# Last expert weights, left-half stores, the slot cast and the first q/k loads rearranged in an attention + soft-MoE kernel

## The chip, the cores and the metric

The kernel runs on one core of a Trainium2 chip. A core has five engines, each with its own in-order instruction queue: TensorE (PE, matmuls; its weight loads are shown as PEld), VectorE (DVE), ScalarE (ACT), GpSimd (POOL) and SyncE (SP). Transfers run on 16 DMA engines that all queues share. A DMA is issued from the queue of an engine (here GpSimd, ScalarE or SyncE) and runs on its own afterwards. The metric is the device time in microseconds; all times below are us from the first instruction of the profiled execution unless said otherwise.

## The reference

Attention over 4 batches, 8 heads, 768 positions, head size 64. Three heads are causal, five see a window of 64 and 4 first positions. The result, as 3072 tokens of 512 features, goes through a soft mixture of experts: 32 slots, 4 for each of 8 experts.

```python
scores = scale * np.matmul(q, k.transpose(0, 1, 3, 2))
scores = np.where(mask[None, :, :, :], scores, -1000000000.0)
a = np.exp(scores - np.max(scores, axis=-1, keepdims=True))
a = a / (np.sum(a, axis=-1, keepdims=True) + 1e-09)
x = np.matmul(a, v)                       # then (3072, 512)
...
logits = x @ phi                          # 3072 x 32
d = softmax of logits over the tokens;  slot_input = d.T @ x
for e in range(E):                        # 8 experts, 4 slots each
    h = np.maximum(slot_input[e] @ w1[e], 0.0)
    slot_out[e] = h @ w2[e]
c = softmax of logits over the slots
return (c @ slot_out).astype(np.float32)  # 3072 x 512
```

Inputs are float32; the kernel computes in bfloat16 with float32 sums and writes float32.

## The kernel before

The order of instructions on each engine is written out by hand (`manual_schedule`). Work falls into four stages.

**Start.** The first pair of heads of q and k goes by two plain float32 loads into the tile `stage`: q from ScalarE's queue and k from SyncE's (L264). VectorE casts q to bfloat16 and ScalarE casts k (L291, L292), TensorE transposes k and then q, and the two engines bring them back as `Tk` and `Tq`. All later inputs and weights are loaded by GpSimd, which casts to bfloat16 in the transfer; they share one in-order queue: q, k, v of four heads at a time, and between them the sixteen weight matrices w1[0..7], w2[0..7] (`w_load`, L142), 2 MB of float32 each.

**Attention.** Sixteen rounds of one pair of heads (`for n in range(NP)`): scores on TensorE, exp on ScalarE (L185), masks on VectorE (L197), products with v on TensorE (L206), normalization on VectorE. It ends near 110 us.

**Slots and experts.** Logits, slot sums and the first expert layer (L528, w1), the transposes of its result (`turn`), and the second layer. `second(e, xs, spread)` (L560) does w2[e] in eight matmuls for each column half x in `xs`: half 0 is columns 0 to 255 ("left"), half 1 is 256 to 511 ("right"), summed over experts in the PSUM tiles `sp[0]` and `sp[1]`. w2[5], w2[6] and w2[7] go into buffers that attention sets free: w2[5] into the masks', w2[6] and w2[7] into the two buffers of `pT`. `w_half(e, cs)` (L429) loads one column half of w2[e]. GpSimd's queue ends with: w2[5] whole, then left halves of w2[6] and w2[7], then right halves of w2[6] and w2[7]. Each half row of 256 bfloat16 is its own piece of 512 B in the destination.

**Output.** Every partition holds 24 output rows. `product(r, o, cs, t)` multiplies row set r with columns cs of `slot_out` (L584) and scales it out of PSUM: with t == 2 on ScalarE (L586), else on VectorE (L588). Once the left halves of all w2 are in, VectorE casts `sp[0]` to `slot_out[:, left]` (L599), and `half_rows` computes and stores the left half of rows 0 to 7, in groups of 2, 2 and 4 rows, from GpSimd's queue (L596). TensorE then does the right half of w2[6], three filler matmuls (`keep_busy`, L280, on zeros), and the right half of w2[7]. VectorE casts `sp[1]` to `slot_out[:, right]` (L604), and rows 8 to 23 follow whole: row 8 as two halves on both engines, the others in turn on ScalarE (odd rows) and VectorE (even rows), stored from SyncE's queue in groups of 1, 1, 2, 4, 4, 4 rows (L616). Last come the right halves of rows 0 to 7, in two groups of 4, on SyncE's queue. The output tiles lie in the buffers of w1.

Of the kernel before, what the change touches and what calls it, by code (L numbers as in the profile page):

```python
# [10 lines left out]
F32 = mybir.dt.float32  # L11
# [27 lines left out]
def kernel(  # L39
# [13 lines left out]
    nc = tc.nc  # L53
    P = 128
# [3 lines left out]
    NE, DM, F = moe_w1.shape  # L58
# [16 lines left out]
    def single(shape, dt, name, tag=None):  # L75
        return singles.tile(shape, dt, name=name, tag=tag or name)

    w1s = [single([P, 4, F], BF16, f"w1_{e}") for e in range(NE)]
    w2s = [single([P, 8, DM], BF16, f"w2_{e}") for e in range(NE - 3)] + [None] * 3
# [55 lines left out]
    w2v = [moe_w2[e].rearrange("(fi fo) d -> fi fo d", fo=8) for e in range(NE)]  # L135
# [83 lines left out]
    def x_transpose(n, i0=0, i1=6):  # L219
        b, hp = n // 4, n % 4  # L220
        tp = trp.tile([P, S], BF16, tag="tr", name="tpx")
        for i in range(i0, i1):
            nc.tensor.transpose(tp[:, i * 128:(i + 1) * 128], xb[b][:, i, hp * 128:(hp + 1) * 128], ident)  # L223
        nc.vector.tensor_copy(xT[:, hp, i0 * 128:i1 * 128], tp[:, i0 * 128:i1 * 128])  # L224
# [35 lines left out]


    stage = ptp.tile([P, 2, S], F32, tag="pT", name="stage")
    for eng, src, z in ((nc.scalar, q, 0), (nc.sync, k, 1)):
        eng.dma_start(stage[:, z], src[0, 0:2].rearrange("h (p s) d -> (h p) (s d)", s=12))  # L264
    ir32 = is_retrieval.tensor.reshape([H]).bitcast(I32)
    nc.sync.dma_start(ri, bass.AP(tensor=ir32, offset=0, ap=[[0, 1], [1, 2 * H]]))
    raws[0] = raw.tile([P, 2, 2 * S], BF16, tag="raw", name="raw")
# [6 lines left out]
    V = nc.vector  # L274
# [3 lines left out]
    def keep_busy(t, count):  # L278
        for _ in range(count):
            nc.tensor.matmul(t, zero[:, :P], zero, start=True, stop=True)  # L280

    idle = pvp.tile([P, 512], F32, tag="pv", name="idle")
# [55 lines left out]
    for n in range(NP):  # L338
# [18 lines left out]
        m, x = (1, 0) if n == 1 else (n // 2 + 1, n % 2)  # L357
        turns = 0 < n < NP - 2
        b, r = n // 4 - 1, n % 4
# [67 lines left out]
    left, right, full = slice(0, 256), slice(256, 512), slice(0, 512)  # L427

    def w_half(e, cs):  # L429
        nc.gpsimd.dma_start(w2s[e][:, :, cs], w2v[e][:, :, cs])  # L430
# [1 line left out]
    w2s[5] = single([P, 8, DM], BF16, "w2_5", tag="msk")  # L432
    nc.gpsimd.dma_start(w2s[5], w2v[5])
    w2s[6] = ptp.tile([P, 8, DM], BF16, tag="pT", name="w2_6")
    w_half(6, left)


    def bank(t, shape=(P, 512), dt=F32):
        pool, tag = ((scp, "sc"), (trp, "tr"), (pvp, "pv"))[t]
        return pool.tile(list(shape), dt, tag=tag, name="bank")  # L440
# [28 lines left out]
    logits_mm(bl, (0, 1, 2))  # L469
    w2s[7] = ptp.tile([P, 8, DM], BF16, tag="pT", name="w2_7")  # L470
    w_half(7, left)
    for e in (6, 7):
        w_half(e, right)
    x_transpose(last, 0, 3)
    x_transpose(last, 3, 6)
    copies(2, 0)
    idle = bank(2)
# [15 lines left out]
    idle = bank(2)  # L493
# [22 lines left out]
    cs = bank(1, (P, 1))  # L516
# [5 lines left out]
    for e4 in range(2):  # L522
        t = xp.tile([P, 2, 512], BF16, tag="xb", name="hs")
# [26 lines left out]

    spt = [bank(0, (P, 2, 512)) for x in range(2)]
    sp = [t[:, 0, :256] for t in spt]
    idle = spt[1][:, 1]

    def second(e, xs=(0, 1), spread=False):
        e4, g = e // 4, e % 4
        for fo in range(8):
            c = fo % 4 if spread else g
            for x in xs:
                nc.tensor.matmul(sp[x][32 * c:32 * c + 32, :], hT[e4][:, fo, 32 * g:32 * g + 32],  # L560
                                 w2s[e][:, fo, 256 * x:256 * x + 256],
                                 start=(e4 == 0 and fo == 0), stop=(e == 7 and fo >= 4))
# [9 lines left out]
    turn(1)  # L572
    second(4, spread=True)
    second(5, spread=True)
    for e in (6, 7):
        second(e, (0,), spread=True)


    NL = 8
    ov = out.rearrange("(p r) d -> p r d", r=24)  # L580

    def product(r, o, cs, t):
        op = bank(t, (P, cs.stop - cs.start))
        nc.tensor.matmul(op, er[r], slot_out[:, cs], start=True, stop=True)  # L584
        if t == 2:
            nc.scalar.activation(o, op, ACT.Copy, scale=rrow[:, r:r + 1])  # L586
        else:
            V.tensor_scalar(o, op, rrow[:, r:r + 1], None, op0=ALU.mult)  # L588

    def half_rows(cs, t0, groups, banks, eng):  # L590
        ot, r = single([P, NL, 256], F32, f"oh{t0}", tag=f"w1_{t0}"), 0
        for rows in groups:
            for _ in range(rows):
                product(r, ot[:, r], cs, banks[r % len(banks)])
                r += 1
            eng.dma_start(ov[:, r - rows:r, cs], ot[:, r - rows:r])  # L596

    slot_out = single([P, DM], BF16, "slot_out", tag="slot_bf")
    V.tensor_copy(slot_out[:, left], sp[0])  # L599
    half_rows(left, 0, (2, 2, 4), (1, 2), nc.gpsimd)  # L600
    second(6, (1,), spread=True)
    keep_busy(idle, 3)
    second(7, (1,), spread=True)
    V.tensor_copy(slot_out[:, right], sp[1])  # L604
    r = NL
    for z, groups in enumerate(((1, 1, 2), (4,), (4,), (4,))):
        ot, base = single([P, 4, DM], F32, f"ot{z}", tag=f"w1_{4 + z}"), r
        for rows in groups:
            for _ in range(rows):
                if r == NL:  # L610
                    for t, cs in ((1, left), (2, right)):
                        product(r, ot[:, 0, cs], cs, t)
                else:
                    product(r, ot[:, r - base], full, (1, 2)[r % 2])
                r += 1
            nc.sync.dma_start(ov[:, r - rows:r, :], ot[:, r - rows - base:r - base])  # L616
# [36 lines left out]
```

## Time and profile before

| What | Value |
|---|---|
| median of 7 runs | 155.65 us (155.15 to 156.19) |
| the profiled execution | 155.68 us, of which its span of instructions is 153.9 us |
| busy: PE, PEld, DVE, ACT, POOL | 79%, 50%, 69%, 71%, 24% of the span |
| read from HBM, written to HBM | 52.49 MB, 6.29 MB: 382 GB/s over the span |
| GpSimd's queue (q0) | 26.91 MB written by its packets, 34064 packets |
| chain that ended last | DMA 16%, PE 6%, ACT 6%, DVE 3% |
| loads of whole w matrices | 1024 KB landed each, issue to landing 13.5 to 33.3 us |
| the first loads of q and k | 384 KB each, 4.6 and 4.4 us from issue to landing |

How to read it: a busy share is an average over the four stages, which have different limits, so the views by stretch of time say more than the totals. Bytes of a DMA are counted at its destination: a weight matrix is 2 MB read and 1 MB written. The share of the DMA engines can be over 1.00 where packets overlap. The granted clock is the part of TensorE's full clock that it was given in that stretch.

### The profile page before, as it was taken

What the parts mean: (1) busy time and instruction counts of PE and PEld (TensorE: products, weight loads), DVE (VectorE), ACT (ScalarE), POOL (GpSimd) and SP (SyncE); (2) the same over time, 40 slices, a digit from 0 to 9 for tenths busy, and PEclk for the clock granted to TensorE, in tenths of its full rate; (3) what the DMA queues carried; (4) which work ended last, traced back from release to release, by engine and by line L of the source; (5) the groups of instructions that cost most, each with busy time, mean ns of one, the idle gap of its engine ahead of it and who ended that gap; (6) DMA issues with size and microseconds to landing.
All of it is one profiled execution on the core that took longest, in us unless ns stands there. A gap on an engine that the chain in (4) does not pass through costs nothing. (4 is left out here: it accounts for less than half of the span.)

```text
span 153.9 us, 5038 instructions
## 1 busy us (share of the span) xinstructions
PE 121.2 (79%) x2236; PEld 77.2 (50%) x2236; DVE 106.2 (69%) x247; ACT 109.9 (71%) x148; POOL 36.5 (24%) x54
## 2 busy tenths in 40 slices
PE   6657997868797989988889989778988997779400
PEld 2324564655565666665566666545535485334200
DVE  1299688999988779989688898779735132439600
ACT  3468698969799899999999999999351131429600
POOL 7970200372116052052036200000360000500000
PEclk9999999999999999999999999999999599758955
DMA  4999999999999999999999999999999999959995
GB/s 149 193 195 223 181 201 187 219 200 182 215 197 226 173 215 217 177 221 200 180 220 202 189 218 219 213 215 215 215 217 217 204 189 199 193 201 375 409 384 195
DMA packets 36295, 33.25 MB, mean 216 GB/s; under 512 B 26034, under 2 KB 31410, under 8 KB 34098
## 3 DMA queue, kind: packets, MB, share of 16 engines
q0 software_dynamic: 34064, 26.91, 110.5%
q1 hardware_dynamic: 2066, 5.64, 9.6%
q10 hardware_dynamic: 144, 0.39, 0.7%
q8 instruction: 17, 0.28, 0.7%
q14 instruction: 4, 0.03, 0.1%
HBM read 52.49 MB, written 6.29 MB: 382 GB/s over the span
## 5 line engine op out<-in xcount | busy, mean ns | idle before, releaser
L185 ACT ACTIVATE pT<-sc 128x1024 bf16<-128x1024 f32 (+1 forms) x96 | 82.6, 938 | 8.0 <-PE sc L180 7.6
L180 PE MATMUL sc<-Tq,Tk 64*128 64x256 bf16 (+3 forms) x320 | 36.7, 293 | 12.1 <-ACT Tk L165 5.4
L206 PEld LDWEIGHTS <-pT 128*128 128x128 bf16 x672 | 24.6, 98 | 11.9 <-issue 7.1
L197 DVE TENSOR_TENSOR pT<-pT,msk 128x1024 bf16<-128x1024 bf16 (+1 forms) x48 | 29.1, 637 | 0.1
L206 PE MATMUL pv<-vb,pT 128*128 128x65 bf16 x352 | 27.2, 195 | 0.3 <-DVE xb L215 0.3
L206 PE MATMUL pv<-vf,pT 128*128 128x65 bf16 x320 | 24.9, 196 | 0.0
L180 PEld LDWEIGHTS <-Tk 64*128 64x128 bf16 x320 | 13.3, 96 | 21.0 <-issue 7.9
L127 POOL DMA_DIRECT2D vb<-in_v_dram x8 | 11.5, 1442 | 42.7 <-PE pv L206 24.9
L151 PEld LDWEIGHTS <-raw 64*64 64x64 bf16 x768 | 16.1, 116 | 10.1 <-issue 7.8
L163 DVE COPY Tq<-tpq 128x768 bf16<-128x768 bf16 x16 | 15.3, 955 | 5.2 <-PE tpq L151 5.1
L215 DVE TENSOR_TENSOR xb<-pv,rs 128x384 bf16<-128x384 f32 x32 | 17.8, 557 | 1.1
L165 ACT COPY Tk<-tpk 128x768 bf16<-128x768 bf16 x16 | 13.0, 815 | 1.6 <-PE tpk L151 1.6
L214 DVE RECIPROCAL rs<-pv 128x6 f32<-128x6 f32 x32 | 6.2, 193 | 8.8 <-PE pv L206 8.6
L151 PE MATMUL tpk<-ident,raw 64*64 64x64 bf16 x384 | 9.7, 201 | 2.7 <-ACT raw L292 1.3
L223 PE MATMUL tpx<-ident,xb 128*128 128x128 bf16 x96 | 8.1, 218 | 2.7 <-DVE Tq L163 1.5
L584 PE MATMUL bank<-slot_out,expR 128*128 128x256 bf16 (+1 forms) x33 | 8.8, 377 | 1.6 <-DVE slot_out L599 0.5
L151 PE MATMUL tpq<-ident,raw 64*64 64x64 bf16 x384 | 10.0, 203 | 0.0
L224 DVE COPY xT<-tpx 128x768 bf16<-128x768 bf16 (+1 forms) x17 | 8.9, 527 | 1.2 <-PE tpx L223 1.2
L586 ACT ACTIVATE ot<-bank,rrow 128x512 f32<-128x512 f32 (+1 forms) x9 | 5.7, 664 | 4.7 <-PE bank L584 4.7
L142 POOL DMA_DIRECT2D w<-in_moe_w_dram x12 | 6.5, 552 | 5.1 <-DMA vb<-in_v_dram 2.5
L223 PEld LDWEIGHTS <-xb 128*128 128x128 bf16 x96 | 6.0, 97 | 3.5 <-issue 3.4
L584 PEld LDWEIGHTS <-expR 128*128 128x128 bf16 x33 | 4.7, 153 | 6.0 <-issue 4.8
(91 smaller groups left out, 113.5 us busy)
## 6 DMA issues: line engine op xcount, KB each, us to landing
w<-in_moe_w_dram POOLq DMA_DIRECT2D x14, 1024.0 KB, 16.9
vb<-in_v_dram POOLq DMA_DIRECT2D x8, 384.0 KB, 11.1
out_dram<-ot SPq DMA_DIRECT2D x3, 1024.0 KB, 5.2
raw<-in_q_dram POOLq DMA_DIRECT2D x7, 384.0 KB, 16.2
raw<-in_k_dram POOLq DMA_DIRECT2D x7, 384.0 KB, 18.1
w<-in_moe_w_dram POOLq DMA_DIRECT2D x4, 512.0 KB, 19.3
out_dram<-oh SPq DMA_DIRECT2D x2, 512.0 KB, 7.1
out_dram<-oh POOLq DMA_DIRECT2D x2, 256.0 KB, 4.1
```

Source lines behind the costliest of these rows:

```text
L127: nc.gpsimd.dma_start(vbs[m % 3].rearrange("p h j d -> p (h j) d")[:, :, :D], v[b, h:h + 4].rearrange("h (j p) d -> p (h j) d", p=P))
L151: nc.tensor.transpose(tp[po, s, :], src[po, 64 * s:64 * s + 64], ident[po, po])
L163: nc.vector.tensor_copy(o, i)
L165: nc.scalar.copy(o, i)
L180: nc.tensor.matmul(sc[:, hh, at:at + 128 * cnt], kT[po:po + 64, j * 128:(j + 1) * 128], qT[po:po + 64, i0 * 128:(i0 + cnt) * 128], start=T ...
L185: nc.scalar.activation(pT[n][:, :, o:o + ln], sc[:, :, :ln], ACT.Exp, scale=scale)
L197: nc.vector.tensor_mul(x, x, m)
L206: nc.tensor.matmul(pv[n][:, i % 3, hh, :], pT[n][:, hh, o:o + 128], vv[:, hh, j, :D + 1], start=(j == 0), stop=(j == i))
L215: nc.vector.tensor_mul(features(xb[b][:, 3 * half:3 * half + 3], n), pv[n][:, :, :, :64], rs.to_broadcast([P, 3, 2, 64]))
L223: nc.tensor.transpose(tp[:, i * 128:(i + 1) * 128], xb[b][:, i, hp * 128:(hp + 1) * 128], ident)
L224: nc.vector.tensor_copy(xT[:, hp, i0 * 128:i1 * 128], tp[:, i0 * 128:i1 * 128])
L584: nc.tensor.matmul(op, er[r], slot_out[:, cs], start=True, stop=True)
```

## The change

- The first k and q are both issued from ScalarE's queue, k first; SyncE's queue begins with the load of `is_retrieval`.
- w2[6] is loaded whole; only w2[7] comes in column halves, left then right.
- TensorE does both halves of w2[6] ahead of the left half of w2[7]. The filler matmuls between the right halves, and the tile they wrote to, are gone.
- A function `take(x)` casts a half of `slot_out` in two pieces of 128 columns: VectorE the first, ScalarE the second.
- The left stores of rows 0 to 7 are issued from SyncE's queue instead of GpSimd's.
- The left half of row 8 is computed on ScalarE ahead of the right half of w2[7]; its right half is done afterwards in two pieces of 128 columns, the first on VectorE and the second on ScalarE. The four tiles of the whole rows are made earlier (`ots`).

```diff
@@ -260,8 +260,8 @@
 
 
     stage = ptp.tile([P, 2, S], F32, tag="pT", name="stage")
-    for eng, src, z in ((nc.scalar, q, 0), (nc.sync, k, 1)):
-        eng.dma_start(stage[:, z], src[0, 0:2].rearrange("h (p s) d -> (h p) (s d)", s=12))
+    for src, z in ((k, 1), (q, 0)):
+        nc.scalar.dma_start(stage[:, z], src[0, 0:2].rearrange("h (p s) d -> (h p) (s d)", s=12))
     ir32 = is_retrieval.tensor.reshape([H]).bitcast(I32)
     nc.sync.dma_start(ri, bass.AP(tensor=ir32, offset=0, ap=[[0, 1], [1, 2 * H]]))
     raws[0] = raw.tile([P, 2, 2 * S], BF16, tag="raw", name="raw")
@@ -432,7 +432,7 @@
     w2s[5] = single([P, 8, DM], BF16, "w2_5", tag="msk")
     nc.gpsimd.dma_start(w2s[5], w2v[5])
     w2s[6] = ptp.tile([P, 8, DM], BF16, tag="pT", name="w2_6")
-    w_half(6, left)
+    nc.gpsimd.dma_start(w2s[6], w2v[6])
 
 
     def bank(t, shape=(P, 512), dt=F32):
@@ -469,8 +469,7 @@
     logits_mm(bl, (0, 1, 2))
     w2s[7] = ptp.tile([P, 8, DM], BF16, tag="pT", name="w2_7")
     w_half(7, left)
-    for e in (6, 7):
-        w_half(e, right)
+    w_half(7, right)
     x_transpose(last, 0, 3)
     x_transpose(last, 3, 6)
     copies(2, 0)
@@ -550,7 +549,6 @@
 
     spt = [bank(0, (P, 2, 512)) for x in range(2)]
     sp = [t[:, 0, :256] for t in spt]
-    idle = spt[1][:, 1]
 
     def second(e, xs=(0, 1), spread=False):
         e4, g = e // 4, e % 4
@@ -572,8 +570,8 @@
     turn(1)
     second(4, spread=True)
     second(5, spread=True)
-    for e in (6, 7):
-        second(e, (0,), spread=True)
+    second(6, spread=True)
+    second(7, (0,), spread=True)
 
 
     NL = 8
@@ -596,19 +594,23 @@
             eng.dma_start(ov[:, r - rows:r, cs], ot[:, r - rows:r])
 
     slot_out = single([P, DM], BF16, "slot_out", tag="slot_bf")
-    V.tensor_copy(slot_out[:, left], sp[0])
-    half_rows(left, 0, (2, 2, 4), (1, 2), nc.gpsimd)
-    second(6, (1,), spread=True)
-    keep_busy(idle, 3)
+    def take(x):
+        V.tensor_copy(slot_out[:, 256 * x:256 * x + 128], sp[x][:, :128])
+        nc.scalar.copy(slot_out[:, 256 * x + 128:256 * x + 256], sp[x][:, 128:])
+
+    take(0)
+    half_rows(left, 0, (2, 2, 4), (1, 2), nc.sync)
+    ots = [single([P, 4, DM], F32, f"ot{z}", tag=f"w1_{4 + z}") for z in range(4)]
+    product(NL, ots[0][:, 0, left], left, 2)
     second(7, (1,), spread=True)
-    V.tensor_copy(slot_out[:, right], sp[1])
+    take(1)
     r = NL
     for z, groups in enumerate(((1, 1, 2), (4,), (4,), (4,))):
-        ot, base = single([P, 4, DM], F32, f"ot{z}", tag=f"w1_{4 + z}"), r
+        ot, base = ots[z], r
         for rows in groups:
             for _ in range(rows):
                 if r == NL:
-                    for t, cs in ((1, left), (2, right)):
+                    for t, cs in ((1, slice(256, 384)), (2, slice(384, 512))):
                         product(r, ot[:, 0, cs], cs, t)
                 else:
                     product(r, ot[:, r - base], full, (1, 2)[r % 2])
```

## The prediction

> **What bounds the kernel now.** I read the chain of waits first, because it names the resource that ends last:
>
> ```profile
> 111.59 23.94 DMA w<-in_moe_w_dram x2
> 135.53 0.04 issue
> 135.57 0.64 PE bank L560 x8
> 136.22 0.02 issue
> 136.24 0.44 DVE slot_out L604
> 136.68 0.05 issue
> 136.72 3.01 PE bank L584 x7
> ```
>
> The columns are start, length and what. The last weight load (right half of w2[7]) lands at 135.53; then follow its eight matmuls, the cast to `slot_out`, the products, and the stores. Before 135.53 nothing but the load matters. Next I asked whether that load waits for its issue or for bandwidth, with the table by stretches (the last three figures are granted clock, DMA share, and GB/s of bytes written):
>
> ```profile
> core 0: us, PE busy (x) PEld busy (x) DVE busy (x) ACT busy (x) POOL busy (x), PEclk, DMA share, GB/s
> 2.00:2.50 0.50, 0.50 (x3) 0.20 (x2) 0.00 (x0) 0.44 (x1) 0.50 (x1) 1.00 0.50 123
> 3.00:3.50 0.50, 0.50 (x3) 0.18 (x2) 0.35 (x2) 0.00 (x0) 0.50 (x1) 1.00 1.00 393
> 114.00:119.00 5.00, 4.42 (x46) 2.50 (x48) 2.25 (x8) 1.38 (x4) 0.21 (x1) 1.00 1.02 215
> 125.00:131.00 6.00, 5.00 (x128) 3.98 (x128) 1.18 (x4) 0.74 (x2) 0.00 (x0) 1.00 1.45 198
> 131.00:133.40 2.40, 1.54 (x15) 0.81 (x13) 1.72 (x4) 1.70 (x4) 1.31 (x2) 0.87 1.06 144
> 137.00:138.50 1.50, 1.50 (x5) 0.63 (x4) 0.53 (x2) 1.13 (x3) 0.00 (x0) 0.50 0.04 14
> 138.50:141.50 3.00, 2.82 (x10) 1.30 (x9) 2.79 (x5) 2.83 (x5) 0.00 (x0) 0.81 0.91 350
> 141.50:149.00 7.50, 2.43 (x12) 1.30 (x10) 3.34 (x7) 3.38 (x7) 0.00 (x0) 0.83 1.03 418
> 149.00:152.00 3.00, 0.00 (x0) 0.00 (x0) 0.00 (x0) 0.00 (x0) 0.00 (x0) 0.50 0.98 326
> ```
>
> From about 3 us to 131 us the DMA engines never run dry (issues lead landings by 10 to 30 us), so compute that starts earlier moves nothing. There are three places to win or lose: the filling of the engines before 3 us; the rate of the last weights (198 GB/s in the stretch of column halves, 215 in whole loads); and the hole at 137.0 to 138.5, where the left stores are done and the first row store, issued at 137.70, has not started. After it the stores need 14 us whatever happens, but their start is set by the products: with the row stores in flight the share is 0.91 until 141.5 and full afterwards.
>
> **The change, part by part.**
>
> *w2[6] whole instead of halves.* Landings: w2[4] at 119.5 (issue 86.25 + 33.3), w2[5] at 124.77 (107.59 + 17.2), then the four halves at 127.0, 129.7, 132.9, 135.5, the last three read from where TensorE resumes (129.78, 132.92, 135.57). 1 MB as halves costs 1.049 MB / 198 GB/s = 5.30 us, whole 1.049 / 215 = 4.88 us: **0.42 us less**, and w2[7] right would land at 135.1. Here a rule speaks against the gain: the Trainium skill, "DMA: Bandwidth & Descriptors", Specifications, gives 512 B as the smallest transfer for line rate. A half row is 256 bf16 = 512 B, so by the rule halves run at full rate and the gain is 0. The two rates above say otherwise; I take 0.42 and keep 0 as the other end.
>
> *Order of the last quarters.* w2[7] left now comes third instead of second, behind 1.5 MB: it lands one half load (2.65 to 2.9) before the end, at 132.2 to 132.5, against 129.74 for the last left piece before. The left half therefore starts 2.5 us later, at half clock (granted 0.50 from 133). Nobody waits for its rows but the store queue and ScalarE; both are followed below.
>
> *The cast by two engines.* It is not parallel: in the built program ScalarE's half waits for VectorE's half. VectorE 128x128 from PSUM: 0.29 (the siT row, L514); ScalarE: no 128-wide copy shown; its 128x768 copy 0.815 and 128x512 0.58 give 0.23 on a line, 0.36 from the 128x256 and 128x512 scaled rows (0.472, 0.688). I take 0.25, nearer the plain copies. Serial: 0.29 + 0.03 + 0.25 = 0.57 against 0.42: **+0.15** for all that needs the whole half.
>
> *Row 8.* Its left product moves ahead of w2[7] right, to ScalarE (0.47, hidden in the wait for the weights); before, it ran at 136.13 beside the cast. Its right half is split into 128 columns, evacuated by VectorE and ScalarE (about 0.35 each instead of 0.47). For row 9 and later this takes only the difference between a 256-wide and a 128-wide matmul at half clock off the pace after the whole cast, about 0.1. From landing to row 9's matmul: before 136.93 − 135.53 = 1.40; after 0.04 + 0.62 + 0.02 + 0.57 + 0.05 + 0.11 = 1.41. **Nothing gained**. Row 8 itself: matmul 0.11, about 0.15 to its end, 0.35, issue: landing + 1.93 against 2.17, so its store goes at 137.0 instead of 137.7.
>
> *ScalarE's queue ahead of the second cast.* With 132.2: matmuls 0.40, cast 0.65 with its waits, first evacuation at 133.8, four at 0.43, row 8 left 0.47: free at 136.0. Needed at 135.1 + 1.0 = 136.1. Covered, by 0.1 only.
>
> *Left stores on SyncE.* GpSimd's queue loses three issues (2.2 us), nothing is behind them. SyncE has nothing before them and row stores behind. A 4-row store of half rows took SyncE 0.69 to 1.26 to issue, so three end by about 137, before row 8 is ready. The 1 MB goes on the wire from about 135.0 (first two rows ready at 134.1, plus the 0.9 from SyncE's issue at 137.70 to the DMA share rising again) at the 326 to 348 GB/s of the right half's stores: until 138.1. So they fill the hole. Row stores follow in order: rows 8 to 11 (1 MB at 410) until 140.6; rows 12 to 15 were issued at 140.70 and by the 0.4 above come at 140.3, on the wire at 141.1. The store queue is thus not the limit; the pace of products is, and **the end moves by the 0.42 of the landing**.
>
> *keep_busy gone* (1.46 us of TensorE, 133.47 to 134.93). The left products, nine at 0.21, take its place. The skill, "TensorE: Matmul & The Clock Gate", Part 1, says an idle window of about 3.4 us halves the clock and a busy one restores it. The row: granted 0.50 from 132.9 to 139.7 although the fillers ran. Both give no difference before 139.7. Were the clock to stay at half for one more window, rows would come every 0.43 while a row's store takes 0.63: no cost.
>
> *k and q on ScalarE's queue.* Adds 0.39 of issue ahead of the table load (done by 2.9, needed at k's cast). k lands sooner (I expect about 4.2 against 5.18), q about when it did; the first exponentials come about 0.5 sooner, worth nothing at the end. What counts is DMA work lost before 3 us, as the weights queue behind it: shares of 0.50 and 0.66 in 2.0 to 3.0 with two queues. If one queue does half as much there, 0.3 us; at most 0.5 with the slower ramp before 2.0; nothing if the ramp is the memory's. In the tail SyncE's queue alone reaches full share at once, so I take 0.05 and keep 0 to 0.5.
>
> **Sum.** −0.42 (whole load) + 0.01 (cast and row 8) + 0.05 (start) = −0.36, rounded with nothing else to −0.4. The profiled execution took 155.68 (span 153.9 and 1.78 around it), the median is 155.65: **155.25**.
>
> **Rivals.**
>
> 1. *The left half comes in the way* (slower). If the whole load is no faster, w2[7] left lands where the third half did, 132.87, and the last at 135.53. Then matmuls at half clock 0.62, cast 0.65, ScalarE's first evacuation at 134.7, four to 136.4, row 8 left to 136.9, its second cast to 137.15, row 9 at 137.3 instead of 136.93: +0.37; with 0.1 to 0.2 lost at the start 156.1 to 156.2. It decides as soon as the two landings lie less than about 3.0 us apart. For it: the margin of 0.1 above, and the third half, which took 3.13. Against it: five whole loads in a row landed 4.8 to 4.9 us apart.
>
> 2. *The store queue is the limit, and the whole hole is gained* (faster). If products come sooner than I think (clock back at full earlier, ScalarE's cast parallel in effect), stores are continuous from 135.0: 1 MB until 138.1, 16 rows 4.19 MB / 418 = 10.0, right half 3.1: 151.2, against 152.25 now (share 0.24 in the 153rd us). −1.0: 154.6. Against it: rows at half clock are 0.43 apart and four are stored together.
>
> 3. *The start costs more* (no change). 0.4 lost before 3 us eats the gain: 155.6. For it: only half share with two queues; against: the tail.
>
> **How the numbers follow.** 0.3% is 0.47 us, what a measurement of this kernel tells from no change: faster is below 155.18, slower above 156.12. Main case 0.50, 154.9 to 155.5: it lies on the border, 0.25 faster and 0.25 same. Rival 2: 0.14, all faster. Rival 1: 0.28, of which 0.25 slower since some loss at the start is likely with it. Rival 3: 0.08, 0.06 same and 0.02 slower. Sums: faster 0.39, same 0.34, slower 0.27. The range takes rival 2's upper part and rival 1: 154.5 to 156.2; the main case alone 154.9 to 155.5.
>
> **What would show it.** Landing of w2[6] 4.9 after w2[5], TensorE resuming for the last weights at 135.1; DMA share near 1 through 137 to 138.5; ScalarE's second cast starting right after VectorE's and not after row 8's left evacuation; row 8's store at about 137.0, the group of rows 12 to 15 at 140.3; share in 2 to 3 us as before. I am wrong if the last weights land at 135.5 or later, if ScalarE comes to its cast after 136.3, or if row stores wait in the queue behind the left half.

## The result, and the profile after

The changed kernel takes 156.68 us (median of 26 runs, 155.76 to 157.71) against 155.65 (61 runs): ratio 1.0069, 95% interval 1.0054 to 1.0084. It is **slower by about 1.0 us**. (The ratios leave out the few runs that are over 1.5% above the fastest of their kernel.) The forecast was 155.25, with a range of 154.5 to 156.2. The profiled execution took 157.71 with a span of 155.6; it is the longest of the 26 runs, so the sizes come from the medians, and the profile shows only where time can go.

The chain of waits of the changed kernel, from the landing of w2[7]'s left half on (start, length, what):

```profile
113.93 19.80 DMA w<-in_moe_w_dram
133.73 0.04 issue
133.78 0.43 PE bank L558 x8
...
134.55 0.27 ACT slot_out L599
134.82 0.04 issue
134.86 1.55 PE bank L582 x6
136.41 0.02 issue
136.44 0.48 ACT oh L584
136.92 0.04 issue
136.96 0.37 PE bank L582
137.33 0.58 PE bank L558 x5
137.91 0.02 issue
137.93 0.30 DVE slot_out L598
```

Before, the chain's transfer was the last one, w2[7] right. Now it is w2[7] left, which lands at 133.73; the last load lands at 136.37 and the chain does not pass through it. After 133.73 come the left products, an evacuation (the copy of a product out of PSUM) on ScalarE that sets a PSUM buffer free, row 8's left product at 136.96, and only then the last matmuls of w2[7] (L558), which start at 137.26 although their data was there 0.9 earlier. TensorE's own rows, first the nine left products, then those matmuls:

```profile
134.86 2.47 PE L582 MATMUL bank<-slot_out,expR 128*128 128x256 bf16 x9 [0.69 <-ACT slot_out L599]
137.26 0.62 PE L558 MATMUL bank<-w,hT 128*32 128x256 bf16 x8
```

What the DMA engines did in the same stretches, changed kernel (the last three figures are granted clock, DMA share and GB/s written):

```profile
133.00:135.00 2.00, 0.54 (x9) 0.40 (x9) 0.29 (x1) 0.27 (x1) 0.00 (x0) 0.97 0.38 50
135.00:137.00 2.00, 1.86 (x9) 1.11 (x8) 1.68 (x4) 1.46 (x4) 0.00 (x0) 0.50 0.08 18
137.00:139.00 2.00, 1.57 (x12) 0.66 (x12) 0.78 (x3) 1.20 (x4) 0.00 (x0) 0.50 1.03 338
139.00:141.00 2.00, 2.00 (x6) 0.83 (x5) 1.17 (x2) 1.62 (x3) 0.00 (x0) 0.50 0.93 330
141.00:143.00 2.00, 2.00 (x7) 0.87 (x6) 1.90 (x4) 1.82 (x3) 0.00 (x0) 0.82 0.94 373
143.00:149.00 6.00, 2.68 (x12) 1.43 (x11) 3.51 (x7) 3.56 (x8) 0.00 (x0) 0.96 0.97 393
```

and the kernel before:

```profile
133.00:135.00 2.00, 1.93 (x11) 0.44 (x11) 0.00 (x0) 0.00 (x0) 1.28 (x2) 0.50 1.04 267
135.00:137.00 2.00, 1.26 (x11) 0.54 (x11) 0.76 (x2) 0.00 (x0) 0.00 (x0) 0.50 0.86 315
137.00:139.00 2.00, 2.00 (x6) 0.80 (x5) 0.93 (x3) 1.63 (x3) 0.00 (x0) 0.50 0.24 90
139.00:141.00 2.00, 1.88 (x7) 0.93 (x6) 1.90 (x3) 1.83 (x4) 0.00 (x0) 0.85 0.98 381
141.00:143.00 2.00, 1.72 (x7) 0.85 (x6) 2.00 (x4) 2.00 (x4) 0.00 (x0) 1.00 0.95 391
```

The hole of 137 to 139 is filled, as forecast. But a larger one has opened at 133 to 137, where the engines that are through with their weights have nothing to store. Adding up what is missing to a share of 1.00 in each stretch from 133 to 149 gives an idle time of 1.94 us before (0.28 + 1.52 + 0.04 + 0.10) and 3.52 after (1.24 + 1.84 + 0.14 + 0.12 + 0.18). The difference, 1.6, is nearly the 1.7 by which the spans differ.

Not all of that is the tail's doing. From the last landing to the end it is 18.4 us before and 19.2 now, 0.8 more; the other 0.8 is that the last load itself landed later (136.37 instead of 135.53). The trace holds sixteen completions for each load, and a load has landed with the last of them. In this execution the sixteenth came 1.35 after the fifteenth already for w2[5], ahead of everything that the change does in the tail; before it was 0.41. a_two_queues (below) shows such a lag too, 1.62, so the one start queue is not needed for it. Where it comes from stays open.

### The profile page after: what moved, and what is told of

The parts are those of the page before. It is cut to its first block, busy times and chain, and to the rows that moved or that the text cites. A ratio compares the mean times of both kernels' runs of the same rounds, so it can differ in the third digit from the quotient of the medians.

```text
span 155.6 us, 5036 instructions
## 1 busy us (share of the span) xinstructions
PE 120.7 (78%) x2234; PEld 77.1 (50%) x2234; DVE 105.6 (68%) x247; ACT 111.0 (71%) x151; POOL 33.1 (21%) x50
## 5 line engine op out<-in xcount | busy, mean ns | idle before, releaser
L582 PE MATMUL bank<-slot_out,expR 128*128 128x256 bf16 (+2 forms) x34 | 9.7, 403 | 1.7 <-ACT slot_out L599 0.7
L169 DVE TENSOR_TENSOR vf<-vb,fmask 128x528 bf16<-128x528 bf16 x16 | 6.8, 425 | 0.0
```

## The experiments

"b" kernels start from the kernel before, "a" kernels from the changed one. Ratios are to the kernel before on the same chip. Idle is the sum just described; it and the span are those of one execution of each run, which can lie off the run's median (b_nl12's profile took 154.41, its median is 155.07).

| Run | What | Ratio, 95% interval | Idle, us | Span, us |
|---|---|---|---|---|
| before | | 1 | 1.94 | 153.9 |
| changed | | 1.0069 (1.0054 to 1.0084) | 3.52 | 155.6 |
| a_two_queues | changed, first loads as before | 1.0060 (1.0035 to 1.0084) | 3.28 | 155.1 |
| b_one_queue | first loads as in the change | 1.0018 (0.9985 to 1.0050) | 2.50 | 154.6 |
| b_late_compute | six more fillers at the start | 0.9997 (0.9973 to 1.0021) | 1.86 | 153.8 |
| b_w6_whole | w2[6] whole, fillers kept | 1.0089 (1.0055 to 1.0122) | 3.12 | 155.0 |
| b_w6_nobusy | the same, no fillers | 1.0093 (1.0058 to 1.0128) | 3.56 | 155.5 |
| b_order | four halves, order 6, 6, 7, 7, no fillers | 1.0110 (1.0074 to 1.0147) | 3.02 | 155.3 |
| b_w6_sync | b_w6_nobusy, left stores on SyncE | 0.9997 (0.9975 to 1.0018) | 2.00 | 153.4 |
| b_left_sync | left stores on SyncE alone | 1.0007 (0.9979 to 1.0035) | 2.70 | 154.0 |
| a2_row8_back | a_two_queues, row 8 as before | 1.0003 (0.9977 to 1.0028) | 2.44 | 154.2 |
| a2_nl4 | a_two_queues, 4 rows in halves | 1.0039 (1.0019 to 1.0059) | 3.34 | 154.5 |
| b_nl12 | 12 rows in halves | 0.9971 (0.9950 to 0.9993) | 0.18 | 152.5 |
| b_nl12_sync | the same, left stores on SyncE | 0.9931 (0.9903 to 0.9959) | 0.24 | 152.4 |

**First: the start or the tail?** Two theories. S: the one start queue makes the loss. L: the left half stands in front of the right half (my first rival).

a_two_queues takes the start of the kernel before into the changed one:

```diff
-    for src, z in ((k, 1), (q, 0)):
-        nc.scalar.dma_start(stage[:, z], ...)
+    for eng, src, z in ((nc.scalar, q, 0), (nc.sync, k, 1)):
+        eng.dma_start(stage[:, z], ...)
```

> The changed kernel with the first loads as before (q from ScalarE's queue, k from SyncE's). Theory S (the one start queue makes the loss): ratio to before 0.997 to 1.000, last weights land near 135.1, q at about 5.4. Theory L (the left half standing in front of the right half makes it): ratio stays at 1.006 to 1.008. Both at once: 1.002 to 1.004.

Measured 1.0060: L. b_one_queue is the opposite edit, in the kernel before.

> The kernel before, with only the first k and q both from ScalarE's queue. Theory S: ratio 1.006 or more, q lands at 7 or later, weights land 0.6 to 1.8 later than before. Theory L: 1.000, whatever q does, because the DMA queue has a backlog. Both: 1.003 to 1.004.

Measured 1.0018, with an interval that holds 1.000 and 1.004: the start costs little or nothing, and how much stays open. S as the main cause is gone. In the profile q landed at 5.8 here and at 7.7 in the changed kernel, so this run does not test a q as late as that. b_late_compute was to show what a late q could cost.

```diff
-    keep_busy(idle, 8)
+    keep_busy(idle, 14)
```

> The kernel before with six more filler matmuls at the start, so that the first exponential comes some 1 to 1.5 us later while no DMA is issued later than before. If the one queue costs through late compute, the ratio is 1.005 to 1.010 and the weights land later. If it costs through the DMA engines themselves (or not at all), the ratio is 1.000 and the last weights land at 135.5 as before.

Measured 0.9997, last weights at 135.25. But the edit did not delay compute. The fourteen fillers ended at 5.73, when ScalarE's cast of k had only just ended (5.62), and the first exponential came at 8.10, before the 9.28 of the kernel before:

```profile
8.10 1.02 ACT L185 ACTIVATE pT<-sc 128x1024 bf16<-128x1024 f32 x1 [1.02 <-PE sc L180]
```

So the run tests nothing, and what later compute costs is not shown. b_w6_whole takes up L in the kernel before:

```diff
-    w_half(6, left)
+    nc.gpsimd.dma_start(w2s[6], w2v[6])
...
-    for e in (6, 7):
-        w_half(e, right)
+    w_half(7, right)
...
-    for e in (6, 7):
-        second(e, (0,), spread=True)
+    second(6, spread=True)
+    second(7, (0,), spread=True)
...
-    second(6, (1,), spread=True)
     keep_busy(idle, 3)
```

> The kernel before with only w2[6] whole, w2[7] in halves after it, TensorE's order fitted to that; casts, row 8, fillers, stores as before. Theory L: the last weights land 0.4 earlier (135.1), but w2[7] left lands near 132.4 instead of 129.7 and the left rows delay the right half: ratio 1.002 to 1.006. Theory S: the load order is a gain, ratio 0.996 to 0.999.

Measured 1.0089, more than L expected and no better than the whole change. The last weights did land earlier (134.86), w2[7] left at 132.42. TensorE came to the last matmuls at 136.55, 1.7 after their data: left products and fillers stood before them.

**Second: TensorE's order or the stores?** Within L, P says that late last matmuls are the price, Q that late left stores are.

b_w6_nobusy drops the fillers (`keep_busy(idle, 3)`) from b_w6_whole.

> The kernel with only w2[6] whole, without the three fillers. Theory P (the last eight w2[7] matmuls land in time but stand on TensorE behind the left products and the fillers): TensorE comes to them 1.1 to 1.3 earlier, at or within 0.6 of the landing, and the ratio to before falls from 1.009 to 1.000 to 1.003. Theory Q (the late left half costs by its stores, which then stand before the row stores): the matmuls come earlier but the ratio stays above 1.006.

The last matmuls came at 135.69, 0.45 after their data, the first row store at 137.81 instead of 138.38, and the ratio did not move: 1.0093. P fails here, and Q as I had put it (row stores waiting behind left stores) is seen: a first row store took 4.0 to land (137.81 to 141.85) instead of 2.1. a2_row8_back undoes only row 8's part in a_two_queues:

```diff
-    product(NL, ots[0][:, 0, left], left, 2)
...
-                    for t, cs in ((1, slice(256, 384)), (2, slice(384, 512))):
+                    for t, cs in ((1, left), (2, right)):
```

> The changed kernel with the first loads on two queues and row 8 as before (its left product behind the right half of w2[7], its right half in one piece). Theory P: the last eight matmuls start 0.4 to 0.5 earlier after their landing than in the changed kernel (0.9 late there), and the ratio falls from 1.006 to 1.003 to 1.004. Theory Q: no change, 1.006.

Measured 1.0003 against 1.0060: the loss is gone, more than P expected. Its TensorE rows:

```profile
132.73 0.40 PE L558 MATMUL bank<-w,hT 128*32 128x256 bf16 x8 [2.71 <-DMA w<-in_moe_w_dram]
133.82 1.96 PE L582 MATMUL bank<-slot_out,expR 128*128 128x256 bf16 x8 [0.69 <-ACT slot_out L599]
135.71 0.62 PE L558 MATMUL bank<-w,hT 128*32 128x256 bf16 x8
```

From the left half's first matmul to the first of the last w2[7] matmuls it is 2.98 here, 3.38 in a_two_queues and 3.48 in the changed kernel (133.78 to 137.26). That is less than half of the 0.9 us by which the ratio moved. From the last landing to the end a2_row8_back and a_two_queues differ even less, 19.0 against 19.1; what differs is that w2[7] left landed at 132.68 instead of 133.37, ahead of anything that this edit touches, with the lag of one completion described above. So the ratio says that row 8's part costs about 0.6%, but how it comes to that much is not shown; and the run undoes two things at once, the early left product and the right half in two pieces. P explains some of it, and Q is not ruled out. a2_nl4 leaves half as many left rows:

```diff
-    NL = 8
+    NL = 4
...
-    half_rows(left, 0, (2, 2, 4), (1, 2), nc.sync)
+    half_rows(left, 0, (2, 2), (1, 2), nc.sync)
...
-    for z, groups in enumerate(((1, 1, 2), (4,), (4,), (4,))):
+    for z, groups in enumerate(((1, 1, 2), (4,), (4,), (4,), (4,))):
...
-    half_rows(right, 2, (4, 4), (1, 2), nc.sync)
+    half_rows(right, 2, (4,), (1, 2), nc.sync)
```

> The changed kernel with the first loads on two queues and only four rows in column halves instead of eight (so four left products and row 8's stand before the last eight matmuls, and half as much is stored as left half). Theory P: the matmuls start at the landing, the first row store 0.8 to 1.0 earlier than in the changed kernel, ratio 0.998 to 1.001, held back only by the hole that fewer left stores leave. Theory Q: also faster, but then the row stores wait for the left stores in the runs with eight rows and go at once here. The trace tells: in Q a row store's time to landing in the changed kernel is longer than in the kernel before (2.1).

The last matmuls started 0.17 after the landing and the first row store went at 137.22, earlier than before; still 1.0039, so late last matmuls are not the whole price. Its DMA share was 0.59 and 0.64 in 135 to 139: the hole that fewer left stores leave was paid for. What all of these have in common is in the table: span less idle time lies between 151.2 and 152.3 in every row, while the spans go from 152.4 to 155.6. **Q in its new form**: the bytes are the same and the DMA engines need nearly the same time for them (within 1.1 us here); what a variant gains or loses is mostly how long they stand idle between the first engine's last weights and the last store. That is a reading of sums, which the runs that follow test. b_nl12 was made to fill the hole of the kernel before:

```diff
-    NL = 8
+    NL = 12
...
     half_rows(left, 0, (2, 2, 4), (1, 2), nc.gpsimd)
+    half_rows(left, 1, (4,), (1, 2), nc.gpsimd, 8)
...
-    for z, groups in enumerate(((1, 1, 2), (4,), (4,), (4,))):
+    for z, groups in enumerate(((1, 1, 2), (4,), (4,))):
...
+    half_rows(right, 3, (4,), (1, 2), nc.sync, 8)
```

> The kernel before with twelve rows in column halves instead of eight: 0.5 MB more of left stores to fill the hole of 137.0 to 138.5, and 0.5 MB more of right half stores in 1 KB pieces at the end (326 to 348 against 418 GB/s: 0.25 to 0.35 longer). If the hole is what the tail can give, ratio 0.994 to 0.998. If the pace of products bounds the row stores whatever goes before, 1.000 to 1.003.

Measured 0.9971, idle 0.18: faster than before. By the medians the gain is 0.45 us for 1.8 us less idle time, so the sum tells the direction better than the size.

**Third: tests of the new form.** b_order keeps the halves and changes only their order, so that left data is late without any whole load (the fillers, which made no difference between 1.0089 and 1.0093, are left out):

```diff
     w_half(6, left)
+    w_half(6, right)
...
-    for e in (6, 7):
-        w_half(e, right)
+    w_half(7, right)
...
-    second(6, (1,), spread=True)
-    keep_busy(idle, 3)
```

> The kernel before with the four halves in the order 6 left, 6 right, 7 left, 7 right (same pieces, same bytes; fillers left out so that nothing stands before the last matmuls). Theory Q, in its new form (what counts is how long the DMA engines stand idle between the first engine's end of its weights, near 131, and the last store): the left stores start at 136.5 to 137.5 instead of 133.4, idle time 4 or more instead of 2.5, ratio 1.010 to 1.015, and worse than w2[6] whole without fillers (1.0093) by the 0.4 to 0.65 that the halves cost. If the whole load is what costs, 1.000 to 1.003.

Measured 1.0110: it is the order that costs, not the whole load. (The idle sum is below the 4 expected.) Its stretches:

```profile
133.00:135.00 2.00, 1.45 (x13) 1.01 (x13) 1.06 (x3) 0.43 (x1) 0.00 (x0) 0.75 0.52 70
135.00:137.00 2.00, 1.84 (x14) 0.65 (x13) 1.67 (x5) 1.38 (x4) 1.56 (x3) 0.50 0.16 56
```

b_w6_sync changes one word of b_w6_nobusy, `nc.gpsimd` to `nc.sync` for the left stores.

> The kernel with w2[6] whole and without fillers, left stores from SyncE's queue instead of GpSimd's. Theory Q: their first packets come 0.9 to 1.1 earlier after the left half's landing (3.2 instead of 4.3), so the ratio falls from 1.009 to 1.000 to 1.004. If the queue does not matter, 1.008 to 1.010.

Measured 0.9997 against 1.0093. The stretches of b_w6_nobusy:

```profile
133.00:135.00 2.00, 1.48 (x14) 0.99 (x7) 1.22 (x3) 0.58 (x2) 0.00 (x0) 0.50 0.34 46
135.00:137.00 2.00, 1.84 (x14) 0.70 (x13) 1.68 (x5) 1.22 (x3) 1.37 (x2) 0.50 0.07 25
```

and of b_w6_sync:

```profile
133.00:135.00 2.00, 1.56 (x7) 1.09 (x7) 1.50 (x4) 0.90 (x2) 0.00 (x0) 0.61 0.27 37
135.00:137.00 2.00, 1.84 (x13) 0.67 (x12) 1.55 (x4) 0.95 (x3) 0.00 (x0) 0.53 0.76 248
```

The last figures are the ones to read: 248 GB/s instead of 25 in 135 to 137. With SyncE the first store was issued 2.1 after the left half's landing (132.47 to 134.56) and its first packet came 0.9 later; with GpSimd 3.0 (132.62 to 135.63) and 1.3. So the part of the change that moves the left stores is a gain of nearly 1% in this order. Two things are not separated: in this profile the clock was 1.00 in 137 to 139 instead of 0.68, and the left stores went out in packets of 1 KB from SyncE and of 4 KB from GpSimd. In the order of before the same word changes nothing:

> The kernel before with the left stores from SyncE's queue alone changed. Theory Q: they start near 132.5 instead of 133.4, on engines that are through with their weights, but on the late engines they now share with the weights instead of queueing behind them: the last weights land up to 0.8 later. The hole before the row stores stays or grows. Ratio 0.999 to 1.004. Rival: 0.996 to 0.999, if the earlier start is all gain.

Measured 1.0007: the stores start earlier (DMA share 1.18 instead of 1.04 in 133 to 135), and the engines are idle that much longer afterwards (0.63 instead of 0.86 in 135 to 137), because the row stores come no sooner; the last weights landed at 135.57, not later. Where there is no hole it pays:

> Twelve rows in column halves (0.997 with GpSimd's queue), with the left stores from SyncE's queue. Theory Q: no hole is left to fill, so an earlier start on the engines that are free gains at most the 0.3 to 0.5 of idle time before the first store, and what the late engines lose takes from it: 0.995 to 0.999.

Measured **0.9931** (0.9903 to 0.9959; 154.41 us), below the lower end of what was expected. It is faster than both kernels. Its stretches:

```profile
133.00:135.00 2.00, 2.00 (x15) 0.84 (x14) 1.58 (x4) 1.77 (x4) 0.00 (x0) 0.53 1.05 267
135.00:137.00 2.00, 1.62 (x14) 0.78 (x13) 0.80 (x2) 0.00 (x0) 0.00 (x0) 1.00 1.04 358
137.00:139.00 2.00, 1.87 (x8) 0.90 (x7) 1.53 (x4) 1.95 (x4) 0.00 (x0) 1.00 0.88 315
```

## Why the prediction was wrong

Put in a row, the ratios walk from the kernel before to the changed one: order and whole load 1.0093, left stores on SyncE 0.9997, cast by two engines 1.0003, row 8's part (left product early, right half split) 1.0060, one start queue 1.0069. Two steps of the five are large losses, one is a large gain, and two cannot be told from nothing.

The step that failed is the path: the prediction let the last load bound the end ("the end moves by the 0.42 of the landing"), and nobody but the store queue and ScalarE wait for the left half. In the changed kernel the chain runs through the left half instead, and TensorE comes to the last matmuls 0.9 after their data. Two terms were put at nothing for that reason, the late left half and row 8's left product. With the left stores on SyncE the first just eats the gain of the whole load (0.9997 in b_w6_sync, where the forecast of 155.25 is 0.9974); the second brings the loss.

- **Order of the last quarters.** The prediction said that nobody waits for the left rows but the store queue and ScalarE, and let the stores run without a break from 135.0. It counted the hole at 137 as the only idle time of the tail. In 133 to 137 of the kernel before, the left stores already ran while the last weights came in (share 1.04 and 0.86); with the left half's data 2.7 us later (129.74 to 132.42 in b_w6_whole) the engines stood idle there. b_order (1.0110) shows it without a whole load. The bill in engine time that my second rival made on the side of the gain, carried through from 131 on, would have shown it.
- **ScalarE "covered by 0.1 only", and row 8.** The right place, the wrong engine. The last w2[7] matmuls stand behind row 8's left product on TensorE, and that product waits for a PSUM buffer. The nine products, put at 0.21 each (1.9), took 2.47, since row 8's had to wait for an evacuation; its store went 2.90 after the last landing, not 1.93. The prediction called row 8's left product hidden in the wait for the weights; undoing row 8's part is worth 0.6% (1.0060 to 1.0003), of which the traces explain less than half. Rival 1 had this side, with 156.1 to 156.2 and 0.28 of the chance, but put the wait at ScalarE's cast. It was too small.
- **Left stores on SyncE.** That they fill the hole is right, and in this order they are worth more than I gave them. But they began 1.9 later than the 135.0 of the sum: first packet at 136.9, mostly since w2[7] left landed at 133.73 and not at 132.2.
- **w2[6] whole, −0.42.** Right in sign: from w2[5]'s landing to the last, 10.76 before and 10.22 in the changed kernel (126.15 to 136.37). In size it is less sure, as left stores ran beside the halves before; between b_order and b_w6_nobusy, where none do, it is 10.87 against 10.69. Nothing of it reached the end, since the last matmuls did not wait for their data any more. The rate of the trace was the better guide than the 512 B of the rule.
- **The cast.** 0.57 forecast for the two serial pieces; measured 0.29 + 0.03 + 0.27. Right; a difference in time could not be told (0.9997 to 1.0003).
- **Fillers.** Without cost or gain, as forecast: 1.0089 with, 1.0093 without. The clock in the stretches of the tail varied from profile to profile, so no more is read from it.
- **The start.** That compute starting later or sooner is worth nothing was not tested, since b_late_compute did not delay it. The forecast for q ("about when it did") does not hold: q landed at 7.7 instead of 5.35, and the first exponential of the changed kernel came at 10.78 instead of 9.28. In its price of 0.05 the step is not contradicted (0.9985 to 1.0050).

Not tried: the cast by two engines alone, row 8's early left product in the order of before or without the split of its right half, and a compute start that is really later.

## What to carry to other kernels

When the DMA engines bound a kernel, count their idle time from the first engine that finishes its loads to the last store, in every stretch and on both sides of a change; a load order that saves transfer time can lose more than it saves, if it delays the data of stores that would have covered the loads' uneven end. Work put "into a wait" on an in-order engine must also fit there with the buffers it needs: ask what stands right behind it, on each engine that it passes, and when its buffer is set free. The store queue that answers soonest paid here where stores, and not products, were what was late. And an experiment's time says something only once its trace shows that the edit moved what it was meant to move.

## What the runs showed of the hardware that was not expected

One start queue filled the engines better than two, and still its second transfer came later. The share in the changed kernel:

```profile
2.00:2.50 0.50, 0.50 (x3) 0.21 (x2) 0.00 (x0) 0.50 (x1) 0.47 (x1) 1.00 0.93 283
3.00:3.50 0.50, 0.50 (x3) 0.18 (x2) 0.31 (x2) 0.00 (x0) 0.50 (x1) 1.00 0.93 350
```

Over 2 to 3 us the two profiles with one queue have shares of 0.98 and 0.99, the twelve with two queues 0.58 to 0.92. k landed at 3.6 instead of 5.2. But VectorE, which casts q, still had to wait:

```profile
7.75 0.56 DVE L291 CAST raw<-stage 128x768 bf16<-128x768 f32 x1 [4.44 <-DMA stage<-in_q_dram]
```

In the DMA records all but the last nine packets of this queue start by 4.3; those nine come one each 0.25 us from 5.4 to 7.4, beside GpSimd's first loads. In b_one_queue the last starts at 5.4. Why they are so late, and why not each time, stays open.

The 16 DMA engines do not finish equal shares together: in the kernel before, the sixteen completions of the last load are spread from 131.9 to 135.5. The rate of the weights begins to fall at 131.5, and their last packet starts at 135.2. That stretch of up to 4 us is what the left stores had been filling.
